# Attention times values in an attention and expert kernel: four products a pair of heads, or three that are added afterwards

## The chip, the cores and the metric

The kernel runs on one core of one Trainium2 chip. The metric is the device time of one execution in microseconds (us); lower is better. Engines are named as in the profile: PE is the matrix engine (PEld its weight loads), ACT the scalar engine, DVE the vector engine, POOL the GpSimd engine, SP the queue of DMA issues.

## The reference

Attention over 8 batches, 8 heads, 576 positions and 64 numbers a head, with keys and values averaged over groups of 8 positions (so 72 of each), and then a feed-forward network over all 4608 tokens.

```python
k_p = k.reshape(B, H, 72, 8, D).mean(axis=3)
v_p = v.reshape(B, H, 72, 8, D).mean(axis=3)
attn = softmax(q @ k_p^T / sqrt(D))          # 576 x 72 for each batch and head
x = (attn @ v_p), heads side by side         # 4608 x 512
h = x @ w_in                                 # 4608 x 2048
out = (h * clip(h + 3, 0, 6) / 6) @ w_out    # 4608 x 512
```

## The kernel before, in words

**Blocks.** The 4608 tokens are cut into ten blocks (512, 256, 384, six of 512, 384). For a block, 16 expert steps follow one another, one for each 128 of the 2048 hidden numbers: `Step.h` (line 782, `psh<-xhi,w`) makes 12 products over the block's x, `relu` and `hi` run on ACT (L790, L798), `gate` and `lo` on DVE (L794, L802), and two steps later `Step.out` (line 813, `pso<-w,ghi`) makes 12 products into four PSUM banks that sum over the steps. Every number goes in as a high part and a low part, so each of these products is three matmuls: high by high, high by low, low by high. The tile `psh` has two banks, taken in turn: a step's products wait until `gate` has read the bank of the step two before.

**Attention beside it.** While block j runs, the attention of block j+1 is worked out in between, in a list of steps that `block_steps` writes and that `Paced.slot` hands out evenly over the block. A step is one of three kinds. `scores` makes the products with the keys (L412), the maximum (L416, DVE), the exponentials (L420, ACT) and the division (L448, L454, POOL). `transposes` turns a tile of 128 tokens (L518, L520) and writes its high part `ahi` (ACT, L529) and its low part `alo` (DVE, L530). Of the 72 values, 64 go through these; the other 8 of each head lie together in `arem` (L540, L541). `av` makes the products with the values for a *part* (the tokens of one batch in one block, T of them) and a pair of heads. A tile at the seam of two batches has two runs of 64 tokens, each written by itself. Every `scores`, `transposes` and `av` takes the next of **two** PSUM banks (`att_bank`), whose tile is called `psa`.

In `av` (L583) the two heads of a pair stand in a block-diagonal matrix `vhi` (and `vlo` for the low parts), with zeros set by POOL (L318). Four matmuls add into one bank, and one ACT copy (L585) takes the sum to `x`:

```python
mms = [(whi[:, p], hi[:, i, o]), (whi[:, p], lo[:, i, o]), (wlo[:, p], hi[:, i, o])]
return mms + [(wrem[:, g, i * P : (i + 1) * P], rem[:, o])]
```

At the end of a block `split_x` splits x into `xhi` (ACT, L561) and `xlo` (DVE, L562), one pair of heads at a time, and the next block's first `h` reads them.

**What sets the order.** Up to the fourth expert step of block 1 a table written by hand (`ORDER`) sets it. Behind that, the framework's scheduler orders each engine's instructions, by times that it works out itself; each engine then runs its list strictly in that order and waits where something isn't there yet.

The parts of batches 2 to 7 have T = 512; 64 and 448; 128 and 384; 192 and 320; 256 and 256; 320 and 192; 384: twelve parts, four pairs of heads each.

Of the kernel before, what the change touches and what calls it, by code (L numbers as in the profile page):

```python
# [17 lines left out]
P = 128  # L18
# [7 lines left out]

SIDE = 12

WSCALE = 2.0**8
# [46 lines left out]
def attention_moe_kernel(  # L76
# [195 lines left out]
    class FirstValues:  # L272
# [24 lines left out]
        def rest(self):  # L297
# [4 lines left out]
            for g in range(NG):  # L302
# [5 lines left out]
                )  # L308

    def place_v(b):  # L310

        W[b] = (
            pool.tile([P, NPAIR, 2 * D], F32R, name="vhi", bufs=2),
            pool.tile([P, NPAIR, 2 * D], F32R, name="vlo", bufs=2),
            pool.tile([3 * REM, NG, 4 * D], F32R, name="vrem", bufs=2),
        )
        for w in W[b][:2]:
            nc.gpsimd.memset(w.bitcast(F32), 0.0)  # L318
# [21 lines left out]
    def place_heads(b, vs):  # L340
        whi, wlo, _ = W[b]
        for h in range(2):
            rows, cols = slice(h * D, (h + 1) * D), slice(h * D, (h + 1) * D)
            hi = whi[rows, :, cols]
            nc.scalar.mul(hi, vs[rows], 1.0 / POOL)
# [167 lines left out]
    def transposes(j, tile, g):  # L513
# [8 lines left out]
        for b, _, n, x0 in tile:  # L522
# [4 lines left out]
            else:  # L527
                hi, lo, _ = a_tiles(j, g)
                nc.scalar.copy(hi[:, :, o], src[:, :2])  # L529
                nc.vector.tensor_tensor(out=lo[:, :, o], in0=src[:, :2], in1=hi[:, :, o].bitcast(F32), op=ALU.subtract)  # L530
# [47 lines left out]
    def av(j, b, x0, T, p, later=None):  # L578
# [11 lines left out]
        low() if later is None else later.append(low)  # L590

    def side_steps(b):

# [15 lines left out]
    def block_steps(j):  # L609
# [4 lines left out]
        def turn():  # L614
            tile, g = todo.pop(0)
            steps.append(([], lambda: transposes(j, tile, g), None, ()))
            if g == NG - 1:
                while left and (left[0][0], left[0][1] + left[0][2]) in [(b, s0 + n) for b, s0, n, _ in tile]:
                    pb, _, T, x0 = left.pop(0)
                    steps.extend(([], lambda p=p, a=(j, pb, x0, T): av(*a, p), "av", (pb,)) for p in range(NPAIR))  # L620

# [214 lines left out]
    nc.gpsimd.memset(half, 0.5)  # L836

    class Paced:

# [8 lines left out]
        def upto(self, m):  # L848
            while self.done < m:
                pre, step = self.steps[self.done]  # L850
                self.done += 1
                for p in pre:
                    p()
                if step:
                    step()

    window.append(len(traced))
# [151 lines left out]
    def run(steps, lag, attention, first_slot=0, preps={}):  # L1009


        n_out = sum(x.t1 - x.t0 for x in steps[max(first_slot - lag, 0) : len(steps) - lag])
        paced = Paced(attention, len(steps) - first_slot + n_out - 4)
        for u in range(len(steps) + lag):
# [42 lines left out]


# [39 lines left out]
```

## Time and profile before

| | |
|---|---|
| median of 3 runs | 921.2 us (921.14 to 922.93) |
| the profiled execution, its own time | 921.88 us |
| its span in the trace | 920.1 us |
| PE busy / weight loads | 908.7 us / 777.7 us |
| DVE / ACT / POOL busy | 456.6 / 461.4 / 81.1 us |
| granted clock of PE | 1.00 |

The span is the stretch that the trace covers; the execution's own time is 1.8 us longer. The rows of PE overlap one another, since matmuls are pipelined: what a matmul takes of PE's time is read from the start of its row to the start of the next, not from its own length.

### The profile page before, as it was taken

The page shows a single profiled execution, that of the slowest core. Times are in us where ns is not written, and L with a number is a line of the kernel's source. Part 1 is how long each engine was busy: PE and PEld are TensorE (multiplying, and loading weights), DVE is VectorE, ACT ScalarE, POOL GpSimd, SP SyncE. Part 2 cuts the span into 40 slices and gives each one's busy share as a digit, 9 for nine tenths or more (in the row PEclk, how much of TensorE's full clock was granted, in tenths as well). Part 3 has the DMA queues.
Part 4 walks back from the last instruction along what each step waited for, and adds up shares of the span by engine and source line. Part 5 has one row for each costly group of instructions (what it writes and reads, how often), then busy time and mean ns, then how long its engine had stood idle before and what let it go on. Part 6 is the DMA issues. An engine that isn't in the chain of part 4 may idle for free.

```text
span 920.1 us, 12711 instructions
## 1 busy us (share of the span) xinstructions
PE 908.7 (99%) x4568; PEld 777.7 (85%) x4568; DVE 456.6 (50%) x916; ACT 461.4 (50%) x1340; POOL 81.1 (9%) x167
## 2 busy tenths in 40 slices
PE   7999999999999999999999999999999999999998
PEld 6888889999888888888888888888888888888997
DVE  6999845475266333833366336633456234332322
ACT  6998666565355434633456344633545344333322
POOL 4100002021000100110011101110101001100000
PEclk9999999999999999999999999999999999999999
DMA  9960204050031002300051004100310010000100
GB/s 306 393 251 0 92 12 121 1 167 18 1 122 50 24 1 83 102 12 6 0 151 51 12 1 142 54 12 1 91 45 20 1 45 14 1 0 4 44 1 35
DMA packets 41935, 57.19 MB, mean 62 GB/s; under 512 B 7568, under 2 KB 23696, under 8 KB 41872
## 3 DMA queue, kind: packets, MB, share of 16 engines
q1 hardware_dynamic: 41728, 56.37, 19.1%
q8 instruction: 36, 0.59, 0.3%
q14 instruction: 27, 0.22, 0.1%
q10 hardware_dynamic: 144, 0.00, 0.0%
HBM read 46.93 MB, written 9.44 MB: 61 GB/s over the span
## 4 chain that ended last, share of the span: by engine, by line
PE 89%; DMA 5%; DVE 3%; ACT 1%; issue 1%; SPq 0%
PE pso L813 41%; PE psh L782 40%; PE psa L412 4%; PE psa L583 4%; DMA raw<-w_in_l 2%; PE psa L518 1%; DMA stage<-vr_l 1%; DMA qt<-q_l 1%; DMA raw<-w_out_l 1%; DVE u L700 1%; DMA stage<-q_l 1%; DVE u L689 0%; DVE w L728 0%; DVE g L794 0%; PE psa L520 0%
## 5 line engine op out<-in xcount | busy, mean ns | idle before, releaser
L782 PE MATMUL psh<-xhi,w 128*128 128x512 f32 (+2 forms) x1288 | 401.9, 372 | 0.3 <-DVE g L794 0.3
L813 PE MATMUL pso<-w,ghi 128*128 128x512 f32 (+1 forms) x1184 | 367.1, 391 | 0.0
L782 PEld LDWEIGHTS psh<-xhi,w 128*128 128x128 f32 x1288 | 237.7, 188 | 36.4 <-issue 0.7
L813 PEld LDWEIGHTS pso<-w,ghi 128*128 128x128 f32 x1184 | 214.2, 188 | 36.0
L782 PE MATMUL psh<-xlo,w 128*128 128x512 f32 (+2 forms) x644 | 237.4, 369 | 0.0
L794 DVE SCALAR_TENSOR_TENSOR g<-g,psh 128x512 f32<-128x512 f32 (+2 forms) x161 | 101.2, 629 | 271.4 <-ACT g L790 270.3
L813 PE MATMUL pso<-w,glo 128*128 128x512 f32 (+1 forms) x592 | 225.9, 386 | 0.0
L790 ACT ACTIVATE g<-psh,small 128x512 f32<-128x512 f32 (+2 forms) x161 | 103.6, 644 | 208.5 <-PE psh L782 192.1
L782 PEld LDWEIGHTS psh<-xlo,w 128*128 128x128 f32 x644 | 121.2, 188 | 18.1
L802 DVE TENSOR_TENSOR glo<-g,ghi 128x512 fp32r<-128x512 f32 (+2 forms) x161 | 102.3, 636 | 61.9 <-ACT ghi L798 60.2
L813 PEld LDWEIGHTS pso<-w,glo 128*128 128x128 f32 x592 | 111.1, 188 | 21.7
L798 ACT CAST ghi<-g 128x512 fp32r<-128x512 f32 (+2 forms) x161 | 92.9, 577 | 69.9 <-DVE g L794 67.3
L420 ACT ACTIVATE e<-psa,mx 128x72 f32<-128x72 f32 x256 | 78.6, 322 | 50.9 <-DVE mx L416 50.2
L448 POOL TENSOR_TENSOR a<-e,sm 128x256 f32<-128x256 f32 x60 | 40.5, 676 | 514.9 <-PE pso L813 180.3
L420 ACT ACTIVATION_READ_ACCUMULATOR e<-psa,mx 128x1 f32 x256 | 52.9, 207 | 0.0
L416 DVE TENSOR_REDUCE mx<-psa 128x4 f32<-128x288 f32 x72 | 32.3, 453 | 29.3 <-PE psa L412 28.8
L412 PEld LDWEIGHTS psa<-kbd,qt 128*128 128x128 f32 x288 | 43.1, 189 | 4.2
L412 PE MATMUL psa<-kbd,qt 128*128 128x144 f32 x288 | 45.5, 285 | 0.0
L585 ACT COPY x<-psa 128x192 f32<-128x192 f32 (+7 forms) x60 | 23.0, 387 | 32.6 <-PE psa L583 32.4
L332 DVE TENSOR_REDUCE vsum<-vst 128x64 f32<-128x512 f32 (+1 forms) x36 | 37.7, 1065 | 2.8 <-DMA vst<-v_l 2.3
L436 DVE TENSOR_SCALAR sm<-sm 128x4 f32<-128x4 f32 x72 | 12.6, 179 | 48.4 <-ACT e L420 45.1
L529 ACT CAST ahi<-psa 128x256 fp32r<-128x256 f32 (+1 forms) x70 | 24.5, 351 | 18.7 <-PE psa L518 9.8
(93 smaller groups left out, 631.3 us busy)
## 6 DMA issues: line engine op xcount, KB each, us to landing
out<-o SPq DMA_DIRECT2D x35, 256.0 KB, 2.3
raw<-w_in_l SPq DMA_DIRECT2D x16, 512.0 KB, 8.4
raw<-w_out_l SPq DMA_DIRECT2D x16, 512.0 KB, 9.0
kst<-k_l SPq DMA_DIRECT2D x28, 288.0 KB, 3.0
qt<-q_l SPq DMA_DIRECT2D x28, 256.0 KB, 3.3
vst<-v_l SPq DMA_DIRECT2D x24, 256.0 KB, 3.2
vst<-vr_l SPq DMA_DIRECT2D x36, 64.0 KB, 1.9
stage<-k_l SPq DMA_DIRECT2D x4, 288.0 KB, 3.8
```

The costliest lines, as they stand in the source:

```text
L332: nc.vector.tensor_reduce(out=vs[:n, p], in_=st[:n, : POOL * D].rearrange("p (o d) -> p d o", o=POOL), axis=AX.X, op=ALU.add)
L412: nc.tensor.matmul(to, qt[:, p, :], kbds[b % 2][:, p, :], start=r == 0, stop=r == last)
L416: nc.vector.tensor_reduce(out=self.mx, in_=self.ps, axis=AX.X, op=ALU.max, negate=True)
L420: nc.scalar.activation(self.e[:, h], self.ps[:, h], AF.Exp, bias=self.mx[:, h : h + 1], accum_out=self.sm[:, h : h + 1])
L448: engine.tensor_tensor(out=self.a[:, : 4 * D].rearrange("p (h s) -> p h s", h=4), in0=e[:, :, :D], in1=sm[:, :, None].broadcast_to([P, 4, D]),
L583: nc.tensor.matmul(ps, l, r, start=n == 0, stop=n == len(mms) - 1)
L782: nc.tensor.matmul(self.ps, l[f][:, c, :], r[:, c, :], start=c == 0 and i == 0, stop=c == NCC - 1 and i == 2)
L790: nc.scalar.activation(self.g, self.ps, AF.Relu, bias=half, scale=1.0 / (6.0 * WSCALE))
L794: nc.vector.scalar_tensor_tensor(out=g, in0=g, scalar=1.0, in1=self.ps, op0=ALU.min, op1=ALU.mult)
L798: nc.scalar.copy(self.ghi, self.g)
L802: nc.vector.tensor_tensor(out=self.glo, in0=self.g, in1=self.ghi.bitcast(F32), op=ALU.subtract)
L813: nc.tensor.matmul(pos, l, r[:, cols], start=f == 0 and i == 0, stop=f == NF - 1 and i == 2)
```

## The change

For batches 2 to 7 (`by_head`) the operands of `av` are laid out differently. `W[b][h]` now belongs to one head: its 128 rows hold the head's values twice, and each row has the high part in the head's own 64 columns and the low part in the other 64. The transposed attention of one head takes the place of `ahi` or `alo`: high part in the head's 64 rows, low part in the 64 rows under it. One matmul then gives (high + low) by high in 64 partitions of the bank and (high + low) by low in the other 64. A pair needs three matmuls, one a head and one for the rest, each into columns or a bank of its own with no sum in PSUM. ACT copies the low half of each head's bank to `x` (L641), DVE adds the high half (L644), and DVE adds the rest's product over it.

Parts with 3 T over 512 columns (T from 192 up) have the first two pairs' head products start right behind the transposes of the first half of the heads, and the rest's products of all four pairs come last. A step of the list holds as many products as fit in a bank: one where T is over 256, two where T is 192 or 256, three where T is 64 or 128.

`transposes` for these batches makes two ACT copies (64 partitions each) and two DVE subtractions where it made one of each, all of ACT's first and then all of DVE's. The values need two more ACT copies a batch and no zeroing by POOL. The last lines bind the order: each attention matmul must stand ahead of the expert matmul that was 24 places behind it as the program was written.

```diff
+LATE = 24
+    def by_head(b):
+        return b > 1
...
-        for w in W[b][:2]:
+        for w in () if by_head(b) else W[b][:2]:
             nc.gpsimd.memset(w.bitcast(F32), 0.0)
...
+            if by_head(b):
+                rest = slice((1 - h) * D, (2 - h) * D)
+                w = W[b][h]
+                hi, lo = w[rows, :, cols], w[rows, :, rest]
+                nc.scalar.mul(hi, vs[rows], 1.0 / POOL)
+                nc.vector.scalar_tensor_tensor(
+                    out=lo, in0=vs[rows], scalar=1.0 / POOL, in1=hi.bitcast(F32), op0=ALU.mult, op1=ALU.subtract
+                )
+                nc.scalar.copy(w[rest], w[rows].bitcast(F32))
+                continue
...
+                    for t, mine, _ in heads:
+                        nc.scalar.copy(t[mine, :, o], src[mine, :2])
+                    for rem, mine in rems:
+                        nc.scalar.copy(rem[: 2 * REM, o], mine)
+                    for t, mine, under in heads:
+                        nc.vector.tensor_tensor(
+                            out=t[under, :, o], in0=src[mine, :2], in1=t[mine, :, o].bitcast(F32), op=ALU.subtract
+                        )
+                    for rem, mine in rems:
+                        nc.vector.tensor_tensor(
+                            out=rem[2 * REM :, o], in0=mine[:REM], in1=rem[:REM, o].bitcast(F32), op=ALU.subtract
+                        )
...
+    def av_by_head(j, b, x0, T, p, some):
+        g, i = p // 2, p % 2
+        cols = slice(x0, x0 + T)
+        x = x_tile(j, "x", F32)[:, p, cols]
+        bank = att_bank()
+        ps = {h: bank[:, n * T : (n + 1) * T] for n, h in enumerate(some)}
+        for h in some:
+            l = W[b][h][:, p] if h < 2 else W[b][2][:, g, i * P : (i + 1) * P]
+            r = a_tiles(j, g)[h]
+            nc.tensor.matmul(ps[h], l, r[:, i, cols] if h < 2 else r[:, cols], start=True, stop=True)
+        for h in some:
+            if h < 2:
+                nc.scalar.copy(x[h * D : (h + 1) * D], ps[h][(1 - h) * D : (2 - h) * D])
+        for h in some:
+            mine = slice(h * D, (h + 1) * D) if h < 2 else slice(None)
+            nc.vector.tensor_tensor(out=x[mine], in0=ps[h][mine], in1=x[mine], op=ALU.add)
...
+                wide = 3 * a[3] > 512
+                if by_head(a[1]) and g == 0 and wide:
+                    steps.extend(by_head_steps(*a, 0, False))
+                elif by_head(a[1]) and g:
+                    steps.extend([] if wide else by_head_steps(*a, 0, None))
+                    steps.extend(by_head_steps(*a, 1, False if wide else None))
+                    for r in range(NG if wide else 0):
+                        steps.extend(by_head_steps(*a, r, True))
...
+    experts = [n for n in range(window[1], len(traced)) if on_pe(n) and n not in beside]
+    for n in beside:
+        after = bisect.bisect(experts, n) + LATE
+        if n >= window[1] and on_pe(n) and after < len(experts):
+            behind(traced[experts[after]], traced[n].name)
```

**First place: PE, the seam tile of block 8's attention, beside block 7's expert steps 9 to 11.** Before, a pair's four products of a part with T = 320 stand side by side (`ahi`, `alo` by `vhi`, `vlo`; `w_770`, `w_955` are the expert weights of steps 7 and 10):

```order
L813 MATMUL pso<-w_770,ghi 128x512 x2
L583 MATMUL psa<-ahi,vhi 128x320
L583 MATMUL psa<-alo,vhi 128x320
L583 MATMUL psa<-ahi,vlo 128x320
L583 MATMUL psa<-arem,vrem 128x320
L813 MATMUL pso<-w_770,glo 128x512
L782 MATMUL psh<-xhi,w_955 128x512
```

Now the last transposes (L536, L538), the second half of step 9's `h` (`w_893`), one head product, three products of an `out`, and step 11's `h` (`w_998`), in the bank that step 9 leaves:

```order
L536 MATMUL psa<-ident,a 128x128 x2
L538 MATMUL psa<-ident,ar 128x128
L856 MATMUL psh<-xhi,w_893 128x512
L856 MATMUL psh<-xlo,w_893 128x512
L856 MATMUL psh<-xhi,w_893 128x512 x2
L856 MATMUL psh<-xlo,w_893 128x512
L856 MATMUL psh<-xhi,w_893 128x512
L638 MATMUL psa<-ahi,vhi 128x320
L887 MATMUL pso<-w_770,ghi 128x512 x2
L887 MATMUL pso<-w_770,glo 128x512
L856 MATMUL psh<-xhi,w_998 128x512
```

The transposes and the head product that reads what they give have moved together: six expert matmuls lie between them now, where before the first product came 23 matmuls behind the last transpose. Step 9's last products have moved to within three `out` products and one head product of step 11's first.

**The same place on ACT and DVE, now.** ACT's copies of the tile's first run, then step 9's `relu` (L864), one head product's copy (L641), the second run:

```order
L552 CAST ahi<-psa 64x2x64
L552 CAST alo<-psa 64x2x64
L554 CAST arem<-psa 64x64 x2
L864 ACTIVATE g<-psh,small 128x512
L641 COPY x<-psa 64x320
```

DVE's subtractions for the same tile, then step 9's `gate` (L868) and a head product's sum (L644):

```order
L556 TENSOR_TENSOR ahi<-psa,ahi 64x2x64
L556 TENSOR_TENSOR alo<-psa,alo 64x2x64
L560 TENSOR_TENSOR arem<-psa,arem 32x64 x2
L868 SCALAR_TENSOR_TENSOR g<-g,psh 128x512
L644 TENSOR_TENSOR x<-psa,x 64x320
```

The lists now have four rows on each engine ahead of the step's `relu` and `gate`, and DVE's first row waits for ACT's copies.

**Second place: PE, the end of block 3's run, the attention of block 4 (T = 448).** Before, two pairs' products, four side by side:

```order
L813 MATMUL pso<-w_1045,ghi 128x512
L583 MATMUL psa<-ahi,vhi 128x448
L583 MATMUL psa<-alo,vhi 128x448
L583 MATMUL psa<-ahi,vlo 128x448
L583 MATMUL psa<-arem,vrem 128x448
L813 MATMUL pso<-w_1045,ghi 128x512
L813 MATMUL pso<-w_1045,glo 128x512
L583 MATMUL psa<-ahi,vhi 128x448
```

Now single products, each in the other of the two banks, with six expert matmuls after each:

```order
L638 MATMUL psa<-ahi,vhi 128x448
L887 MATMUL pso<-w_998,ghi 128x512 x2
L887 MATMUL pso<-w_998,glo 128x512
L887 MATMUL pso<-w_1045,ghi 128x512 x2
L887 MATMUL pso<-w_1045,glo 128x512
L638 MATMUL psa<-alo,vlo 128x448
L856 MATMUL psh<-xhi,w_1145 128x512
L856 MATMUL psh<-xlo,w_1145 128x512
L856 MATMUL psh<-xhi,w_1145 128x512 x2
L856 MATMUL psh<-xlo,w_1145 128x512
L856 MATMUL psh<-xhi,w_1145 128x512
L638 MATMUL psa<-arem,vrem 128x448
```

A bank is now needed again two such groups later; before, a bank took a whole pair.

## Rows read from the trace of the kernel before

**Rows 1.** The page: busy time, PE's slices and the granted clock.
```profile
PE 908.7 (99%) x4568; PEld 777.7 (85%) x4568; DVE 456.6 (50%) x916; ACT 461.4 (50%) x1340; POOL 81.1 (9%) x167
...
PE   7999999999999999999999999999999999999998
...
PEclk9999999999999999999999999999999999999999
```

**Rows 2.** Windows: busy time of each engine in two stretches (instructions in brackets).
```profile
380.00:580.00 200.00, 200.00 (x956) 167.25 (x955) 95.16 (x194) 95.05 (x298) 19.29 (x39) 1.00 0.17 49
580.00:780.00 200.00, 200.00 (x960) 167.32 (x959) 82.82 (x173) 89.06 (x273) 17.60 (x37) 1.00 0.09 28
```

**Rows 3.** The chain that ended last: shares by engine and by line.
```profile
PE 89%; DMA 5%; DVE 3%; ACT 1%; issue 1%; SPq 0%
PE pso L813 41%; PE psh L782 40%; PE psa L412 4%; PE psa L583 4%; DMA raw<-w_in_l 2%; PE psa L518 1%; DMA stage<-vr_l 1%; DMA qt<-q_l 1%; DMA raw<-w_out_l 1%; DVE u L700 1%; DMA stage<-q_l 1%; DVE u L689 0%; DVE w L728 0%; DVE g L794 0%; PE psa L520 0%
```

**Rows 4.** Timeline of PE: starts of a third and a fourth product, five widths.
```profile
246.94 0.39 PE L583 MATMUL psa<-ahi,vlo 128*128 128x512 f32 x1
247.17 0.40 PE L583 MATMUL psa<-arem,vrem 96*128 96x512 f32 x1
...
444.23 0.34 PE L583 MATMUL psa<-ahi,vlo 128*128 128x384 f32 x1
444.40 0.34 PE L583 MATMUL psa<-arem,vrem 96*128 96x384 f32 x1
...
605.74 0.28 PE L583 MATMUL psa<-ahi,vlo 128*128 128x256 f32 x1
605.86 0.28 PE L583 MATMUL psa<-arem,vrem 96*128 96x256 f32 x1
...
509.86 0.28 PE L583 MATMUL psa<-ahi,vlo 128*128 128x192 f32 x1
509.97 0.28 PE L583 MATMUL psa<-arem,vrem 96*128 96x192 f32 x1
...
296.59 0.28 PE L583 MATMUL psa<-ahi,vlo 128*128 128x64 f32 x1
296.70 0.28 PE L583 MATMUL psa<-arem,vrem 96*128 96x64 f32 x1
```

**Rows 5.** Timeline: a tile from its last transpose to DVE, and one product's copy.
```profile
333.81 0.27 PE L520 MATMUL psa<-ident,ar 128*128 128x128 f32 x1
...
334.11 0.37 ACT L529 CAST ahi<-psa 128x256 fp32r<-128x256 f32 x1 [0.45 <-PE psa L520]
...
334.52 0.42 DVE L530 TENSOR_TENSOR alo<-psa,ahi 128x256 fp32r<-128x256 f32 x1
...
334.98 0.26 ACT L540 CAST arem<-psa 64x128 fp32r<-64x128 f32 x1 [0.49 <-DVE alo L530]
...
341.29 0.37 PE L583 MATMUL psa<-arem,vrem 96*128 96x448 f32 x1
...
341.69 0.53 ACT L585 COPY x<-psa 128x448 f32<-128x448 f32 x1 [0.73 <-PE psa L583]
```

**Rows 6.** Groups by line and shape: busy us, mean ns of one, idle before.
```profile
L802 DVE TENSOR_TENSOR glo<-g,ghi 128x512 fp32r<-128x512 f32 x111 | 76.7, 691 | 41.0 <-ACT ghi L798 39.8 <-PE psa L583 0.8
L790 ACT ACTIVATE g<-psh,small 128x512 f32<-128x512 f32 x111 | 76.4, 689 | 157.8 <-PE psh L782 146.8 <-DVE glo L802 10.1
L794 DVE SCALAR_TENSOR_TENSOR g<-g,psh 128x512 f32<-128x512 f32 x111 | 76.1, 685 | 200.6 <-ACT g L790 199.7
...
L530 DVE TENSOR_TENSOR alo<-psa,ahi 128x128 fp32r<-128x128 f32 x14 | 3.9, 283 | 1.2 <-ACT ahi L529 1.2
L529 ACT CAST ahi<-psa 128x128 fp32r<-128x128 f32 x14 | 3.6, 267 | 1.8 <-DVE arem L541 0.6 <-PE psa L520 0.5 <-DVE alo L530 0.4
L540 ACT CAST arem<-psa 64x64 fp32r<-64x64 f32 x14 | 2.9, 207 | 4.8 <-DVE alo L530 2.7 <-DVE arem L541 2.0
L585 ACT COPY x<-psa 128x512 f32<-128x512 f32 x4 | 2.3, 587 | 6.7 <-PE psa L583 6.7
```

More of the change, by code (lines that the diff above doesn't have):

```diff
@@ L1 @@
+import bisect
 from contextlib import ExitStack
@@ L528, in transposes @@
                 hi, lo, _ = a_tiles(j, g)
+                if by_head(b):
+                    heads = [(t, slice(h * D, (h + 1) * D), slice((1 - h) * D, (2 - h) * D)) for h, t in enumerate((hi, lo))]
+                    rems = [(a_tiles(j, r)[2], src[2 * REM * r : 2 * REM * (r + 1), 2]) for r in range(NG if g else 0)]
+                    for t, mine, _ in heads:
[10 more added lines that the diff above has]
+                        )
+                    continue
                 nc.scalar.copy(hi[:, :, o], src[:, :2])
@@ L590, in av, with by_head_steps @@
         low() if later is None else later.append(low)
+    def av_by_head(j, b, x0, T, p, some):
[14 more added lines that the diff above has]
+            nc.vector.tensor_tensor(out=x[mine], in0=ps[h][mine], in1=x[mine], op=ALU.add)
+    def by_head_steps(j, b, x0, T, g, rest):
+        pairs = range(2 * g, 2 * g + 2)
+        some = {None: (0, 1, 2), False: (0, 1), True: (2,)}[rest]
+        n = max(1, min(512 // T, len(some)))
+        for p in pairs:
+            for o in range(0, len(some), n):
+                yield [], lambda p=p, o=o: av_by_head(j, b, x0, T, p, some[o : o + n]), "av", (b,)
     def side_steps(b):
@@ L616, in turn @@
             steps.append(([], lambda: transposes(j, tile, g), None, ()))
[L617 to L620, printed above, removed]
+            ends = [(b, s0 + n) for b, s0, n, _ in tile]
+            full = [(j, b, x0, T) for b, s0, T, x0 in left if (b, s0 + T) in ends]
+            for a in full:
+                wide = 3 * a[3] > 512
[6 more added lines that the diff above has]
+                        steps.extend(by_head_steps(*a, r, True))
+                elif g:
+                    steps.extend(([], lambda p=p, a=a: av(*a, p), "av", (a[1],)) for p in range(NPAIR))
+            if g:
+                del left[: len(full)]
         for t in tiles_of[j]:
@@ L836, in attention_moe_kernel, with on_pe @@
     nc.gpsimd.memset(half, 0.5)
+    beside = set()
+    def on_pe(n):
+        return traced[n].engine == mybir.EngineType.PE
     class Paced:
@@ L853, in upto @@
                     p()
+                mark = len(traced)
                 if step:
                     step()
+                beside.update(range(mark, len(traced)))
     window.append(len(traced))
@@ L1012, in run @@
         n_out = sum(x.t1 - x.t0 for x in steps[max(first_slot - lag, 0) : len(steps) - lag])
-        paced = Paced(attention, len(steps) - first_slot + n_out - 4)
+        paced = Paced(attention, len(steps) - first_slot + n_out - (4 if steps[0].blk.j < 2 else 4))
         for u in range(len(steps) + lag):
```

## The prediction

> **What bounds the kernel now.** I read the page first: PE is busy 99% of the span at granted clock 1.00, its slices are full from the second to the last but one, and DVE and ACT stand at half [rows 1]. Busy PE time alone proves little, since its rows overlap, so the windows by stage come next: in the stretches that hold most of the attention of batches 2 to 7 PE is busy 200.00 of 200 us, DVE 95 and 83, ACT 95 and 89 [rows 2]. The chain that ended last is PE for 89%, 81 of that the experts' two products and 4 the products of `av` [rows 3]. Last the timeline: in these stretches the start of one matmul follows the last at the spacing of its own width, and no PE row waits. So PE's order is full; taking a matmul away saves its spacing, and any wait put in front of a matmul adds itself to the end.
>
> **What is removed.** Twelve parts by four pairs lose one matmul each: 48. Its price is the spacing to the next start: T = 512 0.23 us, 384 0.17, 256 0.12, 192 and 64 0.11 each [rows 4]. Between these I take 448 at 0.20 and 320 at 0.145, and 128 at 0.11. Over the twelve parts: 0.23 + 0.11 + 0.20 + 0.11 + 0.17 + 0.11 + 0.145 + 0.12 + 0.12 + 0.145 + 0.11 + 0.17 = 1.74 us for one pair, 7.0 us for four. Bounds from the same rows: with columns alone counted (0.23 us for 512, so 0.45 ns each, 13,824 columns) it is 6.2; that narrow products stand singly now, between 512-wide ones that can cover their weight loads, can only add some tenths. I take 7.0.
>
> The Trainium skill, "TensorE: Matmul & The Clock Gate", section "Back-to-back issue gap", gives a sustained spacing of about 81 ns for 128 columns and 131 ns for 512. By it an estimate of the saving (its two figures joined by a line) is 4.9 us instead of 7.0. The trace disagrees at both ends, 0.23 us at 512 and 0.11 at the narrow widths [rows 4], so the rows decide.
>
> **What is added off PE.** A pair now takes two ACT copies for one and three DVE sums for none: 48 copies and 144 sums. A copy is 0.53 to 0.59 us at the widest [rows 5, 6]; no trace row shows a sum of 64 partitions out of PSUM. The nearest below is the 128-element subtraction at 0.28, the nearest above the 512-wide one at 0.69 [rows 6]; at the mean width of 288 I take 0.45, so some 65 us of DVE. The transposes add 60 copies and 60 subtractions of at most 0.37 and 0.42 [rows 5]: 22 and 25 us. DVE goes from under half to some 62%, ACT to 55%. That is hidden under PE's full order as total work: cover is gone only if either passes 100%. POOL's twelve memsets were off the path and give nothing.
>
> **What the added work can cost.** Only waits in PE's list count. I counted matmuls in the new order from each producer to its consumer, at the spacings of [rows 4], and set the chain on ACT and DVE against it.
>
> *Transposes to head product.* At three places six expert matmuls lie between (6 x 0.23 = 1.37 us; other places have 2.6 or more). The chain: ACT starts 0.28 to 0.30 us behind the start of the last transpose [rows 5]. Where it stands on a seam tile ACT then makes 2 x 0.27 + 2 x 0.21 = 0.96, and DVE 0.28 for the first head, 0.28 for the second [rows 6]: 1.55 and 1.83 us, against 1.4 to 1.5 available. At a whole tile the copies are 2 x 0.37 + 2 x 0.26 and DVE's 0.42 each [rows 5], so 2.0 and 2.4. Stalls: 0.35 at one seam, 0.85 at the whole tile. At the other seam (the first place shown above) the head product is late by some 0.1 only, but `gate` of step 9 stands behind four DVE rows and behind `relu`: from the start of step 9's last `h` matmul 0.40 until ACT reads [rows 5], then `relu` 0.69 and `gate` 0.69 [rows 6], 1.8 us, and step 11's first matmul comes after 1.06. That is 0.6 to 0.8 there. Together 1.8.
>
> *Two banks for single products.* Behind one product the bank is held 0.40 until ACT starts [rows 5], 0.59 for the copy at T = 512, 0.69 for the sum at most [rows 6]: 1.7 us from its start. The order gives 3.0 or more nearly everywhere (two groups of six matmuls and a product each). One place in block 3's attention has 1.66: 0.1 to 0.2. Elsewhere 1.3 us of slack remain, and an ACT or DVE row of the experts in front takes up to 0.69 of them; two such rows take it all. A few will meet: there are 112 product groups in place of 48, and I put 1 us for all of them, between nothing (no two rows ever meet) and 6 (every second group is late by 0.1).
>
> *The end of a block.* The last rest product now comes up to 2 us behind the next block's first `h` in the list; it needs 0.4 + 0.6 + two split instructions of about 0.65 [rows 6], 2.3 us, and its reader stands 6.6 us behind. Slack 4.3, so nothing. Values and divisions have 35 us and 8 us in the order: nothing.
>
> Sum: -7.0 + 1.8 + 0.2 + 1.0 = -4.0 us. The profiled execution took 921.9, so 917.9 by its own time; the median of the runs is 0.7 lower, so **917.2 us**.
>
> **Rivals.**
> 1. *No stall shows.* The new order could be one whose waits all fall on PE's running ahead in the records by a row. For it: the trace of before shows no wait of PE in these stretches with an order from the same scheduler [rows 2]. Against it: there a bank had at least 4 us, now 1.4 to 3. It gives 921.2 - 7.0 = 914.2, up to 915.4. Chance 0.17.
> 2. *The banks eat the gain.* Each product now needs ACT, then DVE, before its bank is free, and both engines run their lists strictly in order behind `relu`, `gate`, `hi` and `lo`. With 1.8 us from the first kind of place it takes 3.4 us more over 112 groups, 0.03 us a group, to come to within 0.2% of before (919.4 to 923.0). For it: ACT and DVE rise most just at the ends of the blocks, where groups come every 1.57 us. Against it: 2 groups take 3.1 us and a bank is held 1.7. Chance 0.16. [...]
> 3. *Slower.* The same mechanism with a loop: a late sum delays `gate`, which delays the bank of `psh`, which stalls PE for the experts too. Place: the last 20 us of each block's run, seven runs. It decides at 8.8 us, so 1 us for each run more than the 1.8 allowed for; at 1.5 us a run the time is 921.2 - 7.0 + 1.8 + 10.5 = 926.5. For it: in the new order the distance from a step's last `h` matmul to the reuse of its bank falls under 3.1 us at some ten places in mid-block, where before it was over 6 there; `relu` and `gate` take 1.6 of it and one row of attention on either engine up to 0.69 each. Chance 0.10.
>
> **How the numbers follow.** The forecast, stalls of 1.2 to 5.2 us (915.4 to 919.4), has the remaining 0.57. A measurement of this kernel tells some 0.2% (1.8 us) from no change. Faster by more: 0.17 + 0.57 = 0.74; within: 0.16; slower: 0.10. The range goes from the saving without stalls, 914.2, to 920.4, which takes in about a quarter of rival 2: 0.17 + 0.57 + 0.05 = 0.79. The likeliest case alone is 915.4 to 919.4.
>
> **What the profile after would show.** PE 4520 matmuls, 48 fewer, with the other spacings as before. Right: PE idle rows in front of L638 and L856 that name DVE, 2 to 4 us together, largest at the three short distances; DVE near 545 us busy, ACT near 505. Rival 1: no such rows. Rivals 2 and 3: PE waits on DVE L644 in front of L638 in many rows, or on L868 in front of L856, at the blocks' ends. Wrong would be the spacing itself, if the three products in separate banks or columns cost more than 0.11 to 0.23 us each; or waits at places where I count over 3 us of slack, which would mean that ACT or DVE runs a list whose rows wait for one another.

## The result, and the profile after

The changed kernel takes 924.48 us (median of six runs, 923.56 to 926.03) against 921.99 (six runs): 1.0025 times the kernel before, 95% interval 1.0015 to 1.0035. It is slower by a quarter of a per cent; forecast was 917.2. The profiled execution took 923.56 us, with a span of 921.8. The kernel before was measured again beside each group of runs below, and its median there was 921.99 to 922.58, so half a microsecond between two groups says nothing; the changed kernel was measured only here. One run of the kernel before was slow (2752 us) and stands in no ratio.

The page of the changed kernel answers to [rows 1] and [rows 3]: busy time, PE's slices, the granted clock, and the chain that ended last.

```profile
PE 908.0 (99%) x4520; PEld 771.6 (84%) x4520; DVE 544.4 (59%) x1120; ACT 510.8 (55%) x1460; POOL 72.5 (8%) x155
...
PE   7999999999999999999999999999999999999998
...
PEclk9999999999999999999999999999999999999999
...
PE 90%; DVE 4%; DMA 2%; ACT 2%; issue 1%; SPq 1%; DVEq 0%; ACTq 0%
```

48 matmuls are gone, DVE and ACT are about as busy as forecast (545 and 505 us), and PE's slices look as before: the page hides what happened, since 0.7 us of PE's busy time is all that it shows as saved. The windows by stage answer to [rows 2]:

```profile
380.00:580.00 200.00, 199.40 (x941) 164.73 (x940) 120.43 (x254) 108.77 (x328) 16.65 (x36) 1.00 0.16 47
580.00:780.00 200.00, 198.88 (x937) 164.18 (x936) 112.87 (x245) 105.77 (x317) 16.13 (x34) 1.00 0.10 30
```

PE has holes now, 0.60 and 1.12 us. They are the smaller part of a wait, since the row of the matmul ahead reaches into it. The view of waits for weight loads (what waits, for whom: us in total, times, longest), 150 to 900 us, shows more; for the kernel before it is empty there:

```profile
PEld psh L856 <- DVE g L868: 3.1, 5, 1.0
PEld psa L638 <- DVE ahi L556: 2.7, 5, 0.9
PEld psa L536 <- issue: 1.1, 3, 0.4
PEld psa L638 <- issue: 1.0, 4, 0.3
PEld pso L887 <- DVE glo L876: 0.6, 1, 0.6
PEld psa L638 <- DVE x L644: 0.4, 1, 0.4
PEld psa L430 <- ACT e L438: 0.2, 1, 0.2
```

`h` waits for its bank (`gate`, L868), head products wait for the tile's subtraction (L556), `out` once for `lo` (L876). A product waits for a sum (L644) once only. For the rows with `issue` the profile names no releaser.

**What the waits cost.** I went through PE's rows from 100 to 905 us and added up what lies between the start of a matmul and the start of the next beyond the spacing of its width (512 0.232 us, 448 0.205, 384 0.175, 320 0.148, 256 0.120, narrower ones 0.11; 0.105 more from a transpose to another matmul), where that is over 0.025. Left out are gaps of 0.08 to 0.10 us between two matmuls that follow no wait: each kernel has some 115 of them in this stretch, about 10 us in each, and what they are was not looked into. Before, this gives 0.7 us; after, 7.2 in 45 places. With none of these gaps left out it is 11.3 and 17.0, so the difference between the kernels is 5.7 to 6.5 us, by how they are sorted. The largest, 23 of the 45 in twelve places (us from the span's start):

| place, us | who waits for what | cost | forecast |
|---|---|---|---|
| 504 | head product, subtraction on a seam tile | 0.46 | 0.35 |
| 641 | head products, subtractions on a whole tile | 1.12 | 0.85 |
| 714 | head product 0.26, then `h` for `gate` 0.68 | 0.93 | 0.6 to 0.8 |
| 245 | product of block 3's run, for a bank | 0.21 | 0.1 to 0.2 |
| 208 | `h`, `gate` behind subtractions and a sum over keys | 0.90 | none |
| 492 | `h`, `gate` behind `relu` behind exponentials | 0.67 | none |
| 206 | `out`, `lo` behind a sum over keys | 0.43 | none |
| 494, 702 | head products, subtractions on seam tiles | 0.50, 0.33 | none |
| 316, 697, 570 | transposes, for a bank; at 570 `h`, `gate` behind a sum over values | 0.52 together | none |

The third place, 714 us (shown first in the section on the change), in the timeline of the changed kernel, the rows of PE, ACT and DVE:

```profile
713.64 0.40 PE L856 MATMUL psh<-xhi,w 128*128 128x512 f32 x1
714.03 0.42 PE L638 MATMUL psa<-ahi,vhi 128*128 128x320 f32 x1
714.28 0.62 PE L887 MATMUL pso<-w,ghi 128*128 128x512 f32 x2
714.73 0.40 PE L887 MATMUL pso<-w,glo 128*128 128x512 f32 x1
715.54 0.50 PE L856 MATMUL psh<-xhi,w 128*128 128x512 f32 x1 [0.41 <-DVE g L868]
715.87 0.39 PE L856 MATMUL psh<-xlo,w 128*128 128x512 f32 x1
...
713.23 0.43 ACT L554 CAST arem<-psa 64x64 fp32r<-64x64 f32 x2
714.08 0.69 ACT L864 ACTIVATE g<-psh,small 128x512 f32<-128x512 f32 x1 [0.42 <-PE psh L856]
...
713.69 0.28 DVE L556 TENSOR_TENSOR ahi<-psa,ahi 64x128 fp32r<-64x128 f32 x1 [1.78 <-ACT arem L554]
...
714.31 0.45 DVE L560 TENSOR_TENSOR arem<-psa,arem 32x64 fp32r<-32x64 f32 x2
714.80 0.69 DVE L868 SCALAR_TENSOR_TENSOR g<-g,psh 128x512 f32<-128x512 f32 x1
```

The last product of step 9's `h` starts at 713.64; `relu` follows 0.44 behind it, `gate` after `relu`, and step 11's first matmul at 715.54, 0.81 us behind the matmul ahead of it where 0.23 is the spacing. No row of the attention holds these two up: DVE's subtractions end as `relu` does. What is short is the distance in PE's list, as the prediction had it. The next matmul comes 0.33 later and not 0.23: the weight load of the waiting one starts with it, at 715.54, and the next load at 715.65, so the one behind it starts late. The same 0.10 us stands behind the wait at seven of the twelve places and is counted in their cost.

The largest place that I had not foreseen, near 207 us, in the rows of DVE and PE:

```profile
205.32 0.75 DVE L217 TENSOR_REDUCE ksum<-kst 128x72 f32<-128x576 f32 x1 [0.40 <-DMA kst<-k_l]
205.99 0.55 DVE L876 TENSOR_TENSOR glo<-g,ghi 128x384 fp32r<-128x384 f32 x1
206.57 0.42 DVE L556 TENSOR_TENSOR ahi<-psa,ahi 64x256 fp32r<-64x256 f32 x1
207.00 0.43 DVE L556 TENSOR_TENSOR alo<-psa,alo 64x256 fp32r<-64x256 f32 x1
207.44 0.58 DVE L560 TENSOR_TENSOR arem<-psa,arem 32x128 fp32r<-32x128 f32 x2
208.06 0.75 DVE L217 TENSOR_REDUCE ksum<-kst 128x72 f32<-128x576 f32 x1
208.84 0.55 DVE L868 SCALAR_TENSOR_TENSOR g<-g,psh 128x384 f32<-128x384 f32 x1
...
208.32 0.38 PE L536 MATMUL psa<-ident,a 128*128 128x128 f32 x2
209.45 0.44 PE L856 MATMUL psh<-xhi,w 128*128 128x384 f32 x1 [0.75 <-DVE g L868]
```

`relu` was done at 207.25; `gate` started at 208.84, behind three subtraction rows and a sum over the keys that fill DVE without a gap. One of the three (`alo`, 0.43 us) the change has added. At 206 us `lo` stands behind another sum over the keys, for which DVE first waited 0.40 us until the keys had landed; that is nearly the whole loss there (0.43), and the prediction has no such load in its sum.

And 492 and 494 us, where lists wait for one another (ACT, DVE, PE):

```profile
491.37 0.70 ACT L864 ACTIVATE g<-psh,small 128x512 f32<-128x512 f32 x1
492.83 0.62 ACT L872 CAST ghi<-g 128x512 fp32r<-128x512 f32 x1 [0.75 <-DVE g L868]
493.35 0.25 ACT L552 CAST ahi<-psa 64x128 fp32r<-64x128 f32 x1
...
492.11 0.69 DVE L868 SCALAR_TENSOR_TENSOR g<-g,psh 128x512 f32<-128x512 f32 x1
493.48 0.69 DVE L876 TENSOR_TENSOR glo<-g,ghi 128x512 fp32r<-128x512 f32 x1 [0.69 <-ACT ghi L872]
494.20 0.28 DVE L556 TENSOR_TENSOR ahi<-psa,ahi 64x128 fp32r<-64x128 f32 x1
...
492.85 0.50 PE L856 MATMUL psh<-xhi,w 128*128 128x512 f32 x1 [0.41 <-DVE g L868]
...
494.54 0.35 PE L638 MATMUL psa<-ahi,vhi 128*128 128x192 f32 x1
```

The tile's transposes started at 489.78, 4.8 us ahead of the product. ACT copies them only at 493.35, behind four exponentials, `relu`, and `hi`, for which ACT stands idle 0.75 us until `gate` is done; DVE subtracts behind `lo`, for which it waits for `hi`. At 702 us the same: the transposes started at 697.92, the product at 702.51, and ACT copied the tile only at 701.53, behind four exponentials.

### The profile page after: what moved, and what is told of

It is laid out like the page before. It is cut to its first block, busy times and chain, and to the rows that moved or that the text cites. A ratio compares the mean times of both kernels' runs of the same rounds, so it can differ in the third digit from the quotient of the medians.

```text
span 921.8 us, 13014 instructions
## 1 busy us (share of the span) xinstructions
PE 908.0 (99%) x4520; PEld 771.6 (84%) x4520; DVE 544.4 (59%) x1120; ACT 510.8 (55%) x1460; POOL 72.5 (8%) x155
## 4 chain that ended last, share of the span: by engine, by line
PE 90%; DVE 4%; DMA 2%; ACT 2%; issue 1%; SPq 1%; DVEq 0%; ACTq 0%
PE psh L856 41%; PE pso L887 41%; PE psa L430 4%; PE psa L638 2%; PE psa L536 1%; DMA raw<-w_in_l 1%; DMA raw<-w_out_l 1%; DVE vsum L340 1%; PE psa L618 1%; ACT e L438 1%; DVE g L868 0%; PE psa L538 0%; DMA vst<-v_l 0%; DVE alo L556 0%; DVE ahi L556 0%
## 5 line engine op out<-in xcount | busy, mean ns | idle before, releaser
L887 PE MATMUL pso<-w,ghi 128*128 128x512 f32 (+1 forms) x1184 | 358.9, 390 | 0.0
L887 PE MATMUL pso<-w,glo 128*128 128x512 f32 (+1 forms) x592 | 221.2, 387 | 0.2 <-DVE glo L876 0.2
L864 ACT ACTIVATE g<-psh,small 128x512 f32<-128x512 f32 (+2 forms) x161 | 103.9, 645 | 139.3 <-PE psh L856 121.2
L868 DVE SCALAR_TENSOR_TENSOR g<-g,psh 128x512 f32<-128x512 f32 (+2 forms) x161 | 101.1, 628 | 134.0 <-ACT g L864 131.9
L876 DVE TENSOR_TENSOR glo<-g,ghi 128x512 fp32r<-128x512 f32 (+2 forms) x161 | 102.9, 639 | 45.4 <-ACT ghi L872 43.7
L644 DVE TENSOR_TENSOR x<-psa,x 64x384 f32<-64x384 f32 (+13 forms) x144 | 65.2, 455 | 58.4 <-ACT x L641 40.7
L641 ACT COPY x<-psa 64x384 f32<-64x384 f32 (+7 forms) x96 | 37.9, 394 | 55.9 <-PE psa L638 54.8
L556 DVE TENSOR_TENSOR ahi<-psa,ahi 64x256 fp32r<-64x256 f32 (+1 forms) x60 | 23.5, 391 | 39.9 <-ACT arem L554 30.2
L552 ACT CAST ahi<-psa 64x256 fp32r<-64x256 f32 (+1 forms) x60 | 20.5, 342 | 36.5 <-PE psa L538 18.5
```

The costliest lines, as they stand in the source:

```text
L641: nc.scalar.copy(x[h * D : (h + 1) * D], ps[h][(1 - h) * D : (2 - h) * D])
L644: nc.vector.tensor_tensor(out=x[mine], in0=ps[h][mine], in1=x[mine], op=ALU.add)
L864: nc.scalar.activation(self.g, self.ps, AF.Relu, bias=half, scale=1.0 / (6.0 * WSCALE))
L868: nc.vector.scalar_tensor_tensor(out=g, in0=g, scalar=1.0, in1=self.ps, op0=ALU.min, op1=ALU.mult)
L876: nc.vector.tensor_tensor(out=self.glo, in0=self.g, in1=self.ghi.bitcast(F32), op=ALU.subtract)
L887: nc.tensor.matmul(pos, l, r[:, cols], start=f == 0 and i == 0, stop=f == NF - 1 and i == 2)
```

## Experiments

Theory A: the 48 matmuls are worth the forecast 7 us, and PE's new waits take them back, each at its place and each because an engine's list holds a row that PE needs behind rows that it does not. Rivals were set against it run by run. Every edit also gives the scheduler another list, and one number of the order rule alone moves the time by 3.7 us (below); a gain of 2 to 4 us is therefore no proof of a reason until the rows at the place show it. "Waits" below is the sum of the method above (100 to 905 us).

| kernel | median us | ratio to before, interval | waits us |
|---|---|---|---|
| before | 921.99 | | 0.7 |
| changed | 924.48 | 1.0025 (1.0015 to 1.0035) | 7.2 |
| three in a bank | 915.36 | 0.9922 (0.9910 to 0.9934) | 0.8 |
| a fourth product | 931.45 | 1.0095 (1.0079 to 1.0110) | 8.8 |
| heads later | 921.95 | 0.9995 (0.9986 to 1.0003) | 6.1 |
| heads first | 922.03 | 0.9999 (0.9990 to 1.0008) | 5.3 |
| rule at 30 | 920.82 | 0.9988 (0.9979 to 0.9997) | 4.9 |
| rule at 36 | 922.60 | 1.0006 (0.9997 to 1.0015) | 6.5 |
| no rule | 949.69 | 1.0299 (1.0285 to 1.0313) | 33.0 |
| heads later, rule at 30 | 920.86 | 0.9982 (0.9974 to 0.9991) | 5.0 |
| no sums | 921.07 | 0.9987 (0.9978 to 0.9996) | 5.5 |
| heads later, experts in turn | 925.21 | 1.0028 (1.0019 to 1.0038) | 9.3 |
| experts in turn | 933.17 | 1.0116 (1.0102 to 1.0130) | 17.5 |
| before, experts in turn | 924.08 | 1.0020 (1.0011 to 1.0029) | 3.0 |
| gate first | 926.17 | 1.0042 (1.0030 to 1.0055) | 9.7 |
| gate first, rule at 30 | 926.34 | 1.0037 (1.0023 to 1.0051) | 9.8 |

### What a matmul is worth: three in a bank, and a fourth product

The kernel before, its products of batches 2 to 7 without high `a` by low values:

```diff
+            mms = mms[:2] if b > 1 else mms
```

> The kernel before with one matmul of each pair's sum taken out for batches 2 to 7 (the high part of a by the low part of the values, so their low part doesn't enter the result); copies, sums, transposes and everything else as before. It asks what 48 matmuls are worth when nothing is added. Theory A (the price was right, the gain goes into PE waits in the new order): 7.0 us less than before, about 915.0, and PE without waits in the middle of the run. Theory B (the price was too high, because weight loads or something beside PE set the pace): 3 us less or fewer, 919 or more.

The changed kernel, the rest's product made twice:

```diff
-            nc.tensor.matmul(ps[h], l, r...)
+            for _ in range(1 + (h == 2)):
+                nc.tensor.matmul(ps[h], l, r...)
```

> The changed kernel with the product of the rest issued twice into the same place, so that a pair again has four matmuls, 48 more in all, at the same widths; the result is unchanged. Theory A: the added matmuls cost their spacing, 7.0 us, less what they put between producers and consumers (at most 1 us): 930 to 931.5. Theory B (PE is no longer the bound, ACT and DVE pace the blocks' ends): at most 3 us more, 927.5 or less.

Without the 48 matmuls, and with nothing else changed, the time falls by 6.85 us against the kernel before as measured beside it (922.21); putting 48 back into the changed kernel adds 7.0, of which 1.6 are more waits. PE has no more waits in the first than before (0.8 and 0.7; its windows by stage):

```profile
380.00:580.00 200.00, 200.00 (x951) 166.86 (x951) 96.86 (x194) 95.95 (x301) 19.14 (x38) 1.00 0.16 48
580.00:780.00 200.00, 200.00 (x952) 166.99 (x951) 81.85 (x173) 88.24 (x271) 16.69 (x34) 1.00 0.09 28
```

The saving is as large as forecast, by the first run; the second agrees with it less closely once its waits are taken off (5.4). The loss lies in the rest of the change.

### From the transposes to a head product: heads later, and heads first

Wide parts' head products all come behind the second half's transposes:

```diff
-                if by_head(a[1]) and g == 0 and wide:
-                    steps.extend(by_head_steps(*a, 0, False))
-                elif by_head(a[1]) and g:
-                    steps.extend([] if wide else by_head_steps(*a, 0, None))
+                if by_head(a[1]) and g:
+                    steps.extend(by_head_steps(*a, 0, False if wide else None))
```

> The changed kernel, but the head products of the first two pairs no longer start behind the first half's transposes; all head products come behind the second half's, the first pairs first. In the new order the shortest way from a transpose to its head product has 3.4 us of matmuls in place of 1.4. Theory A1 (the waits sit where a head product follows its transposes too closely): these waits, some 3 us, go, about 921.5. Theory A2 (the waits come from the two banks and the expert tile's bank, wherever ACT and DVE rows meet): no gain, 923.5 to 925.5.

In `transposes`, the heads' copies and subtractions ahead of those for the rest:

```diff
-                    for rem, mine in rems:
-                        nc.scalar.copy(rem[: 2 * REM, o], mine)
                     for t, mine, under in heads:
                         ...
+                    for rem, mine in rems:
+                        nc.scalar.copy(rem[: 2 * REM, o], mine)
```

> The changed kernel, but in the transposes of batches 2 to 7 the heads' copies and subtractions stand ahead of those for the rest. Theory A: the chain from a tile's last transpose to a head product is shorter by two copies, 0.42 to 0.52 us, so the waits of products behind the subtractions (2.7 us together in the changed kernel) fall to under 1.2; one expert bank now comes back after 0.83 us, which costs up to 1.0, so the time is 922.3 to 924.0 us. Rival C (those waits come from other rows in front of the copies): the waits behind the subtractions stay above 2.2 us, the time at 924 to 925.

Each is 2.5 us faster than the changed kernel; the second came 0.3 us below theory A's range. With the heads later no weight load of a product waits for a subtraction, as theory A1 has it; other waits came, though, and all together fell only from 7.2 to 6.1. With the heads first that wait fell from 2.7 to 0.3, but the one for `gate` stayed at 3.2. The 714 us place of that kernel, rows of PE and ACT, shows why:

```profile
712.10 0.31 PE L638 MATMUL psa<-ahi,vhi 128*128 128x320 f32 x1
712.25 0.63 PE L887 MATMUL pso<-w,ghi 128*128 128x512 f32 x2
712.72 0.39 PE L887 MATMUL pso<-w,glo 128*128 128x512 f32 x1
714.03 0.50 PE L856 MATMUL psh<-xhi,w 128*128 128x512 f32 x1 [0.93 <-DVE g L868]
...
712.12 0.43 ACT L558 CAST arem<-psa 64x64 fp32r<-64x64 f32 x2 [0.68 <-DVE alo L554]
712.57 0.69 ACT L864 ACTIVATE g<-psh,small 128x512 f32<-128x512 f32 x1
```

The head product no longer waits (0.15 us to the next start, the forecast spacing of 320 columns), and `h` waits 1.1 us in place of 0.6: PE is there 0.26 earlier, and `relu`, behind the rest's copies, which now wait for DVE, starts 0.7 and not 0.44 behind the last product of step 9's `h` (711.87). The wait has changed hands within one step.

### How far the order may be moved: 30, 36 and no rule

One number of the changed kernel, in three runs:

```diff
-LATE = 24
+LATE = 30        (36; 10**6)
```

> The changed kernel with 30 in place of 24 in the rule that binds attention matmuls. Nothing else differs, but the scheduler's list has another set of distances: 1.7 us at the shortest place for the bank of h (0.8 with 24), 1.8 us from transposes to product (1.4), 2.5 us for an attention bank (1.4). Theory A (waits sit at the short distances of the list that happens to come out): 919 to 921. Theory C (the added rows cost by their number): as the changed kernel, 924 to 925.

> The changed kernel with the order rule at 36 places in place of 24 (30 took 920.8, none 949.7). Theory A: by the distances (one tile at 1.37 us, two at 2.1, an expert bank after 1.34 and three after 1.7 to 1.8) the waits are 3.5 to 5 us, 919.5 to 921.5 us, as for 30. Rival E (the looser the rule the more the products bunch at the blocks' ends, steadily): 923 to 930 us.

> The changed kernel without the rule that an attention matmul must stand ahead of the expert matmul 24 places behind it. The scheduler then lets the products drift: at the ends of blocks four to eight of them stand with 0.1 us between the uses of a bank, elsewhere 5 us and more. Theory A1 (the rule makes the short distances, and so the waits): the waits in mid-block go, new ones of some 1.5 us for each product stand at three or four blocks' ends: 921 to 928, the waits all at the ends. Theory A2 (waits are spread over ACT and DVE rows that meet anywhere): within 1.5 us of the changed kernel, with waits in mid-block.

30 is 3.7 us faster than 24, 36 is 1.9 faster, and without the rule the time is 25 us longer. For 36 the expectation was missed by 1.1 us, for none by far: there the products bunch at the ends of the blocks, and PE waits up to 4.4 us for `gate`. PE's granted clock was 0.50 in four stretches behind long waits, 23.9 us together with PE busy for 22.4; an estimate from these is that up to 11 of the 25 us are the clock. So this order needs the rule, and between 24 and 36 its number decides which places are short, with no trend. Theory C, by which 30 would have stayed at 924 to 925, is refuted.

### Heads later with the rule at 30

> The head products of wide parts come only behind all transposes, as in the run with the heads later, and the order rule reaches 30 places in place of 24. Theory A (the loss is a sum of short distances, place by place): in this order the shortest stretch from a tile's last transposes to its product is 2.05 us, against 1.37 in the changed kernel, one expert bank comes back after 0.68 us (1.1 us of wait), all others after 1.6 or more; the keys' place near 207 us keeps 0.8. With waits of 3 to 4 us together it takes 919.0 to 920.5 us, and no wait of a product behind a subtraction is over 0.3 us. Rival B (any order loses some 5 us, because every product now needs ACT and then DVE): 920.5 to 922.5 us.

The order with the longest distances is no faster than 30 alone, as far as can be told: 920.86 against 920.82, ratios 0.9982 and 0.9988 with intervals that overlap. It lies 0.36 above theory A's range and inside rival B's, and its waits are 5.0 us where theory A had 3 to 4. The waits for the subtraction are down to 0.2, as theory A wanted, and the two places that it named cost what it said (208 us 0.89, the bank that comes back after 0.68 us 1.05). The other 2 us, 0.35 to 0.5 each near 206, 292, 379, 386 and 736 us, stand where the distances, counted in matmuls, are longer: what else ACT and DVE have in their lists there does not show in them.

### Without DVE's sums

In the changed kernel no high half is added (left out of x), and ACT copies the rest's product over x:

```diff
-            nc.vector.tensor_tensor(out=x[mine], in0=ps[h][mine], in1=x[mine], op=ALU.add)
+            if h == 2:
+                nc.scalar.copy(x, ps[h])
```

> The changed kernel without DVE's sums: the high half of a head's product is not added, and the rest's product is copied over x by ACT, so this part of the computation is left out. Theory A: each bank is free after ACT alone and DVE has some 65 us less, so the waits of the expert products behind the gate shrink (4.7 us together in the changed kernel, under 2.5 here); the waits behind the subtractions at the places with 1.37 us stay, some 0.6 us each. 919.5 to 921.5 us. Rival D (the sums matter little, the loss is the transposes' chain and the order alone): 923 to 925 us.

3.4 us are won back, and 5.5 us of waits stay, with 60 us less on DVE and 18 more on ACT. Waits for `gate` fell from 3.1 to 1.5 (the 4.7 of the expectation adds up two views of the same waits, PE's 1.6 and its weight loads' 3.1); those for the subtractions stayed (2.3). The time lies in theory A's range, but its reason is not shown: in the changed kernel no sum stands right ahead of `gate` on DVE at any of the five places where `h` waits for it. At 714 us that wait went because the new list has a second head product ahead of `h`, which waits in its place (0.40 us), and near 208 us it is as long as before. What the sums cost, apart from the new list, stays open.

### The experts' matmuls held in the order written

```diff
+    for m, n in zip(experts, experts[1:]):
+        behind(traced[n], traced[m].name)
```

was added to the kernel with the heads later, to the changed kernel, and (with the order rule) to the kernel before.

> The kernel of the third experiment (all head products behind the second half's transposes), and the experts' matmuls are held in the order in which the program writes them, so that no half of a step's h drifts behind the next ones. In its order every distance is long: 3.7 us from transposes to product, 2.7 us between uses of an attention bank, 3.2 us from a step's h to the reuse of its bank. Theory A (the gain of 7 us went into waits at short distances): nearly all waits go, 915 to 916.5, below both kernels. Theory C (the added ACT and DVE rows slow PE anywhere, by their number): 919 or more.

> The changed kernel with the experts' matmuls held in the order in which the program writes them, and nothing else: the bank of h is again free 3 us ahead, but some eight head products follow their transposes by six matmuls or fewer. Theory A1 (most is lost at transposes to product): 921 to 923, the remaining waits in front of L638-type rows that name the subtractions. Theory A3 (most is lost at the bank of h, behind gate): 917 to 919.

> A control: the kernel before with both rules on the order (24 places, and the experts' matmuls in the program's order). Its distances hardly change. If the rules themselves do nothing: within 0.1% of before, 922. If holding the experts in turn gives a gain of its own, it shows here and has to be taken off the fifth and sixth experiment.

Both kernels with three products missed theory A, the first by some 9 us, the second by 10 and more. The third shows that the two rules together cost 1.7 us on the kernel before (922.42 beside it), with transposes and `out` waiting; the rule at 24 places alone was not put on that kernel, so what it costs there is not known. My idea was that the scheduler moves the experts' products badly; held in turn, all three kernels wait longer (9.3 against 6.1, 17.5 against 7.2, 3.0 against 0.7). The first lies in theory C's "919 or more" too, but the holding adds to it, and the run at 30 speaks against C.

### Gate first

```diff
+    for e in (mybir.EngineType.Activation, mybir.EngineType.DVE):
+        own = [n for n in range(window[1], len(traced)) if traced[n].engine == e and n not in beside]
+        for n in beside:
+            ahead = bisect.bisect(own, n) - 1 - 2
+            if traced[n].engine == e and n >= window[1] and ahead >= 0:
+                behind(traced[n], traced[own[ahead]].name)
```

> The changed kernel plus a rule for ACT and DVE: a row of the attention stands behind the experts' rows on its engine, but for the last two, that were written ahead of it. Near 207 us the gate then stands ahead of a tile's subtractions and of a sum over the keys. Theory A (the waits of expert products there and near 492 and 714 us come from attention rows in front of the gate): the wait near 207 us, 0.9 us in the changed kernel, is under 0.3, the waits of expert products behind the gate together under 2.5 us in place of 4.7, and the time 921.5 to 923.5 us. Rival F (what the gate gains, the subtractions and sums of the attention lose): the place near 207 us goes, as much appears in front of head products, and the time stays at 924 to 925.5 us.

> The same rule for ACT and DVE, with the order rule of PE at 30 places in place of 24 (30 alone took 920.8). In this order every expert bank comes back after 1.7 us or more and every attention bank after 2.5 or more; one tile has 1.37 us to its product. Theory A: the wait near 207 us (0.8 in the run with 30 alone) is under 0.3, all waits together 3 to 4 us, and the time 919.0 to 920.3 us. Rival F: waits stay at 5 us, 920.4 to 922 us.

They came out 2.7 and 6.0 us above theory A's ranges, and above rival F's too. Near 207 us the wait is as long as before, now 205 us into the span (DVE, then PE, of the first of the two):

```profile
203.70 0.42 DVE L556 TENSOR_TENSOR ahi<-psa,ahi 64x256 fp32r<-64x256 f32 x1
204.13 0.43 DVE L556 TENSOR_TENSOR alo<-psa,alo 64x256 fp32r<-64x256 f32 x1
204.59 0.75 DVE L217 TENSOR_REDUCE ksum<-kst 128x72 f32<-128x576 f32 x1
205.37 0.56 DVE L868 SCALAR_TENSOR_TENSOR g<-g,psh 128x384 f32<-128x384 f32 x1
...
204.70 0.41 PE L536 MATMUL psa<-ident,a 128*128 128x128 f32 x2 [0.51 <-DVE alo L556]
205.98 0.45 PE L856 MATMUL psh<-xhi,w 128*128 128x384 f32 x1 [0.76 <-DVE g L868]
```

A sum over the keys is still ahead of `gate`, and the edit could not move it: the program issues the sums over keys and values ahead of an attention step and does not note them in `beside`, so the rule counts them with the experts' rows. Only the subtractions of the rest now stand behind `gate`; the expectation was wrong on the edit itself. The transposes now wait too, 0.7 us, for the bank that the subtractions read. PE has lost 1.6 us there, in place of 1.3 at 206 and 208 us. This rule on ACT's and DVE's rows passes the wait on and makes more of them (9.7 us). That rows ahead of `gate` on DVE are the cause at 207 us is what the rows show; no run took that wait away, so the cause is not shown by experiment.

## Why the prediction was wrong

**What bounds the kernel** was read rightly: PE's order is full, and a wait put in front of a matmul adds itself to the end. Median less waits is 914.6 for three in a bank, and 915.6 to 917.3 for the twelve kernels with the new operands and three products a pair, while their medians run from 920.8 to 949.7.

**What is removed**, 7.0 us: 6.9 measured with three in a bank; with a fourth product 7.0, or 5.4 without its added waits. The estimate of 4.9 from the Trainium skill, "TensorE: Matmul & The Clock Gate", section "Back-to-back issue gap", is too low for these products, as [rows 4] had it.

**What is added off PE**: 144 sums of 0.455 us (65.2 us; forecast 0.45 and 65), DVE 59% and ACT 55% busy. As total work it is hidden, as forecast. The 62% that the prediction gives for DVE does not follow from its own sum, the 545 us named further down does.

**What the added work can cost** is the part that failed: 3.0 us forecast, 6.5 measured (7.2 less the 0.7 of the kernel before; 5.7 with no gap left out). The four places named were right in place and cause, and nearly in size: 2.7 us against 2.0. The mis-sized term is "I put 1 us for all of them", for rows of ACT or DVE that meet elsewhere, under *Two banks for single products*: the other eight places cost 3.4 us, 22 small ones 1.1. That term was for attention banks, and what went wrong lay mostly elsewhere: `h` and `out` behind a late `gate` or `lo` at 208, 492 and 206 us took 2.0, head products behind a late copy at 494 and 702 took 0.8, and for these the sum had no term of their own. I had counted each producer and consumer against PE's list, and walked ACT's and DVE's lists only at the named places; rival 3 pointed to "some ten places in mid-block" and I left it at 0.10. But the stall is not the one that rivals 2 and 3 feared: one product waits for a sum, 0.4 us. What is late is `gate`, `relu` and `lo`, mostly behind rows that the change did not add (sums over keys or values, exponentials), or a tile's copies behind these. That this comes from the scheduler's new order and not from the added rows is argued, not shown: every run has both.

**"With the other spacings as before"** failed too, by little: where nothing waits (under 0.3 us), the next matmul starts 229.54 ns behind a 512-wide expert matmul on average after, 229.08 before; over 2626 of them that is 1.2 us. With three in a bank it is 229.12 and without DVE's sums 229.51, so neither the missing matmuls nor the sums make it; what does stays open.

Summed against the profiled execution of before: 921.9 - 7.0 + 6.5 + 1.2 = 922.6, and 923.6 was measured. At 100 us the changed kernel has started two matmuls fewer (489 against 491), half a microsecond; the other half stays open (1.3 by the lower count of waits), and so does why the median lies 0.9 above the profiled run. The last step of the prediction had a fault of its own: "the median of the runs is 0.7 lower" rests on three runs, and with six the median before is 921.99, 0.1 above the profiled execution. So the 7.3 us between forecast and measurement are 3.5 of waits, 1.2 of spacing, 1.0 of the rest, 0.7 of this step and 0.9 of the last median.

**Rivals.** The time lies in rival 3's part, slower by more than 0.2%, which had a chance of 0.10, though 2 us under its 926.5. Its loop of late sums at the blocks' ends is not what happened; the ground that it gave, a short way to the bank of `psh` in mid-block with a row of attention in front of `relu` or `gate`, is what 208 and 492 us show. Rival 1 is refuted by the waits. Of what I had named as proof against me, "waits at places where I count over 3 us of slack, which would mean that ACT or DVE runs a list whose rows wait for one another" came true at 494 and 702 us, with 4.8 and 4.6 us in the list.

**A version that beats both.** The rule at 30, with or without the heads later, takes 920.8 us: 0.12 and 0.18% under the kernel before, with both intervals below 1. These are the two best of eleven orders tried, and the gain is near what can be told at all. Of the 7 us saved, 1.3 to 1.6 arrive.

## What to carry to other kernels

When the bound engine's list is full, an edit that takes work from it and gives work to engines at half load is priced by the waits that it makes, and these must be counted for every consumer that shares the engines' lists, the untouched ones above all: the allowance for rows that meet was 1 us, and they cost 3.4 in eight places. Busy shares did not show it; the view of waits did in seven lines. Where a scheduler writes the order, a change is two changes, its own and a new order: try the order's own knob (here 24 against 30, 3.7 us) before judging the idea.

## What the runs showed of the hardware

In the kernel without the rule the granted clock fell behind long waits of PE, at 373, 565, 582 and 773 us, and the price of the wait went on. Two of these places, in windows of 6.0, 5.0, 6.0, 4.5 and 4.5 us (the last columns are the granted clock, DMA share and GB/s):

```profile
560.00:566.00 6.00, 3.64 (x13) 2.13 (x11) 2.67 (x6) 3.97 (x9) 0.00 (x0) 0.88 0.77 263
566.00:571.00 5.00, 5.00 (x14) 3.69 (x15) 5.00 (x8) 2.16 (x4) 0.00 (x0) 0.50 0.42 131
571.00:577.00 6.00, 5.66 (x30) 4.70 (x28) 5.94 (x13) 3.90 (x21) 0.00 (x0) 0.97 0.62 177
577.00:581.50 4.50, 0.31 (x4) 0.10 (x2) 4.31 (x12) 4.38 (x17) 1.84 (x4) 1.00 0.72 201
581.50:586.00 4.50, 4.50 (x13) 3.50 (x14) 2.51 (x7) 2.10 (x11) 1.04 (x2) 0.62 0.01 2
```

In the first PE stood still for 1.7 us and made a dozen matmuls in all; in the second it works without a gap, at clock 0.50 (1.2 GHz), and makes 14 matmuls in 5 us; in the 5 us from 555 it made 25 at 1.00. In the fourth it is idle for 4.2 us, and the same follows. The waits of the changed kernel, up to 1.0 us, left it at 1.00 from 100 to 905 us.
